# The 16-bit low products of features A, issued once for four steps of a block instead of once for two

## Chip, core and metric

The kernel runs on one core of one Trainium2 chip. The metric is the device time in microseconds (us) of one execution. TensorE (PE in the profile, PEld for its weight loads) multiplies matrices, VectorE (DVE) and ScalarE (ACT) work elementwise, GpSimd (POOL) adds and issues some transfers, and SyncE (SP) issues most transfers. Each engine takes its instructions in its own order.

## Reference

```python
def _attn_ref(x, weight):                  # x: 8 x 4096 x 192, weight: 8 x 7
    w = softmax(weight, axis=-1)           # 7 taps for each head of 24 features
    # causal convolution over the sequence: 6 zeros are padded ahead of it
    out = np.einsum('hk,bskhg->bshg', w, x_unf)
    return out.reshape(B, S, D)

def _moe_ref(x, w_in, w_out, s, b):        # x: 32768 x 192
    h = x @ w_in                           # 192 x 2048
    r = np.maximum(h, 0.0)
    g = s * (r * r) + b
    return g @ w_out                       # 2048 x 192

def reference(x, weight, w_in, w_out, s, b):
    return _moe_ref(_attn_ref(x, weight).reshape(32768, 192), w_in, w_out, s, b)
```

So each token's 192 features are smoothed with seven taps, multiplied out to 2048 hidden features, squared where positive, and multiplied back to 192 features.

## The kernel before

**Tiles.** The 32768 tokens are cut into 32 super-blocks `n` of 1024 tokens, and each of these into two blocks `j` of 512. The 2048 hidden features are eight *steps* `p` of 256 in each block. The 192 features are 128 "features A" and 64 "features B". Precision is kept by splitting numbers into a high and a low part: `sA`, `wA`, `tB`, `wB` hold parts of the smoothed tokens, `W` and `WB` parts of the weights, `qh` and `ql` the high and low part of the squared hidden features.

**One step.** `first(n, j, p)` issues 18 matmuls (L659), nine for each half of the rows, into `h`. ScalarE takes the positive part (L674) and squares it (L681) in `q`; VectorE casts `qh` (L683) and subtracts `ql` (L701; from super-block 3 on, `n >= SCALED`, this is 16 bits wide, two steps in one tile). `second(n, j, p)` multiplies `qh` by the output weights: four matmuls on features B (`acc2`, with `WB`), then eight on features A (`acc1`, with `W`), all on L773. The products of the low part `ql` use a 16-bit copy of the output weights, `halves`, which lies in a buffer named `words`: those of features B, `lows_B` (L758), are issued for all eight steps of a block in its last step, and those of features A (L796) are collected in the list `lows_A` and issued for two steps together, in steps 1, 3, 5 and 7. One step's share of L796 is four matmuls, so a visit has eight. All matmuls of a block on features A add into the same two `acc1` accumulators.

**The order of a block.** `first` runs two to three steps ahead of `second` (`LAG = 2`, with one more at a block's start). Written with F for `first`, S for `second`, A for the low products of features A and B for those of features B, TensorE's order from one block into the next is: S7 B A(6,7) of the last block, F2 F3 S0 S1 A(0,1) F4 S2 F5 S3 A(2,3) F6 S4 F7 S5 A(4,5) of this one, then F0 and F1 of the next block with S6 and S7 of this one between, and so on. Below, F3 or S3 is always step 3 of the block in question.

**What else goes on in a block.** VectorE convolves the tokens of the next super-block, piece by piece between the steps (`accA`, `accB`; L237, L239), splits them (L256, L267, L271, L272), and in the second block (j = 1) of a super-block, ahead of step 3's cast, finds the greatest magnitude of the super-block after next (`peak`, L207, until n = 29, since there are 32). That number goes through two GpSimd transfers (`there`, `t`) and returns to VectorE as `m` (L161), ahead of step 7's cast. VectorE's and ScalarE's orders are those of the program text.

**The end of a block.** After S7 and its low products, ScalarE moves the accumulators out (L810, L813), GpSimd adds the two halves of features B (L814, `oB`) and of features A (L818, `oA`), SyncE moves the upper half of `oB` to the lower partitions (L817, into `oC`), and GpSimd adds this to the other half (L823, `oC`); SyncE stores `oA` and `oC`. The order on GpSimd and SyncE isn't fixed by the text: the scheduler that compiles the program sets it by when it reckons that operands come ready.

Of the kernel before, what the change touches and what calls it, by code (L numbers as in the profile page):

```python
# [44 lines left out]
def conv_attention_then_squared_relu_mlp(  # L45
# [98 lines left out]
    def folded(columns):  # L144

        return columns.rearrange("p (a b) -> p b a", a=2)
# [563 lines left out]
    def accumulators(n, j, p):  # L710
        if p == 0:
            acc[n, j] = [ps_o.tile([P, BLK], F32, name=f"acc{k}") for k in (1, 2, 1, 2)[: 4 if n else 2]]
        return acc[n, j]
# [38 lines left out]
    def lows_B(n, j, to, some):  # L752


        for p in some:
            ql = low_halves.pop((n, j, p))
            for k in range(2):
                nc.tensor.matmul(  # L758
                    to[k * DB :][0:DB], halves[1][:, 2 * p + k, :], ql[:, k, :],
                    start=False, stop=p == NPAIR - 1, skip_group_check=True,  # L760
                )

    def second(n, j, p, qh, ql):
        if (n, j, p) == steps[-1]:
            return last(n, j, qh, ql)
        accs = accumulators(n, j, p)

        ends = [NF - 1, NF - 1 if (n, j) != steps[-1][:2] else NF - 3]

        def both(to, w, f, q, start=False, stop=False):  # L770
            for i in range(2):
                r = slice(i * HB, (i + 1) * HB)
                nc.tensor.matmul(  # L773
                    accs[to + 2 * i], w(f, r), folded(q[r, f % 2, :]),
                    start=start and f == 0, stop=stop and f == ends[i],
                )

        scaled = n >= SCALED
        for f in (2 * p, 2 * p + 1):
            both(1, w_outB, f, qh, start=True, stop=scaled)  # L780
            if not scaled:
                both(1, w_outB, f, ql, stop=True)
        for f in (2 * p, 2 * p + 1):
            both(0, loA, f, qh, start=True)
            both(0, hiA, f, qh)
            if not scaled:
                both(0, hiA, f, ql, stop=True)
        if scaled:
            if p == NPAIR - 1 or (n, j, p + 1) == steps[-1]:
                lows_B(n, j, accs[1], range(p + 1))  # L790
            lows_A.append((p, ql))
            if p % 2 or (n, j, p + 1) == steps[-1]:
                for f, low in ((2 * k + c, low[:, c, :]) for k, low in lows_A for c in range(2)):
                    for i in range(2):
                        r = slice(i * HB, (i + 1) * HB)
                        nc.tensor.matmul(  # L796
                            accs[2 * i], halves[0][r, f, :], low[r],
                            start=False, stop=f == ends[i],
                        )
                lows_A.clear()  # L800
        if p == NPAIR - 1:
            t0 = n * SUP + j * BLK
            early = (n, j) == (1, 0)

            sb = tok_s[n]
            o = {}
            for k, name in ((1, "oB"), (0, "oA")):
                o[k] = outs.tile([P, BLK], F32, name=name)
                o[k + 2] = outs.tile([P, BLK], F32, name=name + "2", bufs=1)
                nc.scalar.activation(  # L810
                    o[k], accs[k], AF.Identity, scale=sb, bias=0.0 if early else bias[:, k : k + 1]
                )
                nc.scalar.activation(o[k + 2], accs[k + 2], AF.Identity, scale=sb)  # L813
            nc.gpsimd.tensor_tensor(o[1], o[1], o[3], op=ALU.add)  # L814

            oC = outs.tile([DB, BLK], F32, name="oC", bufs=1)
            nc.sync.dma_start(oC, o[1][DB:P])  # L817
            nc.gpsimd.tensor_tensor(o[0], o[0], o[2], op=ALU.add)  # L818
            toA, toB = outT[0:P, t0 : t0 + BLK], outT[P:D, t0 : t0 + BLK]
            oB = o[1][0:DB] if early else oC  # L820
            if not early:
                nc.sync.dma_start(toA, o[0])
            nc.gpsimd.tensor_tensor(oB, oC, o[1][0:DB], op=ALU.add)  # L823
            if early:
                unbiased.extend(((o[0], toA, 0), (oB, toB, 2)))
            else:
                nc.sync.dma_start(toB, oB)
            del acc[n, j]
# [14 lines left out]
    def last(n, j, qh, ql):  # L843

        accs = accumulators(n, j, NPAIR - 1)
        sb = tok_s[n]
        uA, uB = upper_sums(accs, sb)
        t0 = n * SUP + j * BLK
        for f in (NF - 2, NF - 1):
            nc.tensor.matmul(  # L850
                accs[1], w_outB(f), folded(qh[:, f % 2, :]), start=False, stop=f == NF - 1
            )
        lows_B(n, j, accs[1], (NPAIR - 1,))
        oB = outs.tile([P, BLK], F32, name="oB")[0:DB]
        nc.vector.scalar_tensor_tensor(
            oB, accs[1][0:DB], sb[0:DB], uB, op0=ALU.mult, op1=ALU.add
        )
        nc.vector.scalar_tensor_tensor(
            oB, accs[1][DB:P], sb[DB:P], oB, op0=ALU.mult, op1=ALU.add
        )  # L860
        nc.sync.dma_start(outT[P:D, t0 : t0 + BLK], oB)
        oA = outs.tile([P, BLK], F32, name="oA")
        for f in (NF - 2, NF - 1):
            for w in (loA, hiA):
                nc.tensor.matmul(
                    accs[0], w(f, slice(0, P)), folded(qh[:, f % 2, :]), start=False, stop=False
                )
        for f in (NF - 2, NF - 1):
            nc.tensor.matmul(
                accs[0], halves[0][:, f, :], ql[:, f % 2, :], start=False, stop=f == NF - 1  # L870
            )
        for k, e in enumerate((nc.scalar, nc.sync)):
            c = slice(k * BLK // 2, (k + 1) * BLK // 2)
            nc.vector.scalar_tensor_tensor(
                oA[:, c], accs[0][:, c], sb, uA[:, c], op0=ALU.mult, op1=ALU.add
            )
            e.dma_start(outT[0:P, t0 + c.start : t0 + c.stop], oA[:, c])
# [93 lines left out]
    steps = [(n, j, p) for n in range(1, NSUP) for j in range(2) for p in range(NPAIR)]  # L971
# [56 lines left out]
    for item in queue:  # L1028
        with in_order(nc.vector):
            second(*item)  # L1030
# [44 lines left out]
```

## Time and profile before

| | |
|---|---|
| median of 3 runs | 2053.38 us (2052.86 to 2054.66) |
| the profiled execution | 2054.64 us, its span 2052.9 us |
| TensorE | busy 2042.1 us, 99% |
| VectorE | busy 1789.1 us, 87% |
| ScalarE | busy 1331.6 us, 65% |
| GpSimd | busy 475.8 us, 23% |
| L796, the moved matmuls | 1852 of this form, busy 241.0 us |

Busy time is the union of an engine's instructions. A matmul's row shows some 376 ns, but the halves run beside each other and overlap, so the pace of the matmuls is read from starts of successive groups. In the timeline a row is a run of like instructions: its start, how long it lasts, the engine, the line, and in brackets how long the engine was idle ahead of it and what ended that.

### The profile page before, as it was taken

The page shows a single profiled execution, that of the slowest core. Times are in us where ns is not written, and L with a number is a line of the kernel's source. Part 1 is how long each engine was busy: PE and PEld are TensorE (multiplying, and loading weights), DVE is VectorE, ACT ScalarE, POOL GpSimd, SP SyncE. Part 2 cuts the span into 40 slices and gives each one's busy share as a digit, 9 for nine tenths or more (in the row PEclk, how much of TensorE's full clock was granted, in tenths as well). Part 3 has the DMA queues.
Part 4 walks back from the last instruction along what each step waited for, and adds up shares of the span by engine and source line. Part 5 has one row for each costly group of instructions (what it writes and reads, how often), then busy time and mean ns, then how long its engine had stood idle before and what let it go on. Part 6 is the DMA issues. An engine that isn't in the chain of part 4 may idle for free.

```text
span 2052.9 us, 43220 instructions
## 1 busy us (share of the span) xinstructions
PE 2042.1 (99%) x18404; PEld 1619.3 (79%) x18404; DVE 1789.1 (87%) x2187; ACT 1331.6 (65%) x1460; POOL 475.8 (23%) x352
## 2 busy tenths in 40 slices
PE   9999999999999999999999999999999999999999
PEld 6789877777777777777777787777777777877776
DVE  9888888888888889888889888898888898888975
ACT  8877866566666665666666656656666666566565
POOL 0013232122231222321222312223212233132210
PEclk9999999999999999999999999999999999999999
DMA  5022222121222222221222222122212222221210
GB/s 196 21 52 77 63 60 63 47 68 45 71 60 50 58 57 58 61 58 49 62 53 71 58 52 58 52 63 60 55 53 60 55 69 59 52 59 47 52 42 19
DMA packets 48561, 121.36 MB, mean 59 GB/s; under 512 B 9200, under 2 KB 9456, under 8 KB 48368
## 3 DMA queue, kind: packets, MB, share of 16 engines
q1 hardware_dynamic: 45824, 114.50, 20.1%
q0 software_dynamic: 2400, 3.97, 1.6%
q8 instruction: 144, 2.36, 0.6%
q14 instruction: 49, 0.40, 0.1%
q10 hardware_dynamic: 144, 0.13, 0.0%
HBM read 35.57 MB, written 25.20 MB: 30 GB/s over the span
## 4 chain that ended last, share of the span: by engine, by line
PE 90%; DVE 4%; DMA 3%; ACT 2%; issue 1%; POOL 0%; SPq 0%; DVEq 0%; POOLq 0%
PE h L659 44%; PE acc L773 31%; PE acc L796 10%; PE acc L758 5%; DMA there<-peak 2%; DMA t<-there 1%; DVE ql L688 1%; ACT q L674 1%; ACT q L681 0%; DVE c L405 0%; DVE t L391 0%; DVE accA L239 0%; DVE qh L683 0%; DVE peak L207 0%; DVE W L411 0%
## 5 line engine op out<-in xcount | busy, mean ns | idle before, releaser
L674 ACT ACTIVATE q<-h 128x1024 f32<-128x1024 f32 x496 | 506.1, 1020 | 585.2 <-PE h L659 570.7
L701 DVE TENSOR_TENSOR ql<-q,qh 128x1024 f16<-128x1024 f32 x464 | 610.9, 1317 | 24.7 <-DVE qh L683 0.5
L681 ACT ACTIVATE q<-q 128x1024 f32<-128x1024 f32 x512 | 543.2, 1061 | 14.3
L773 PE MATMUL acc<-qh,W 64*128 64x512 f32 x3960 | 515.9, 376 | 0.4 <-ACT oA L810 0.3
L683 DVE CAST qh<-q 128x1024 fp32r<-128x1024 f32 x477 | 334.4, 701 | 162.6 <-ACT q L681 156.6
L659 PE MATMUL h<-sA,W 64*128 64x512 f32 x3072 | 461.3, 405 | 2.6 <-DVE W L413 1.7
L773 PEld LDWEIGHTS acc<-qh,W 64*128 64x128 f32 x3960 | 377.2, 186 | 52.7 <-ACT oA L810 0.7
L659 PE MATMUL h<-wA,W 64*128 64x512 f32 x3072 | 416.9, 376 | 0.0
L659 PE MATMUL h<-wB,W 64*128 64x512 f32 x1536 | 413.4, 376 | 0.0
L659 PE MATMUL h<-tB,W 64*128 64x512 f32 x1536 | 413.4, 376 | 0.0
L659 PEld LDWEIGHTS h<-sA,W 64*128 64x128 f32 x3072 | 292.5, 186 | 66.8 <-DVE W L413 2.5
L659 PEld LDWEIGHTS h<-wA,W 64*128 64x128 f32 x3072 | 292.8, 186 | 40.0
L239 DVE SCALAR_TENSOR_TENSOR accA<-xA,taps,accA 128x512 f32<-128x512 f32 x348 | 312.8, 899 | 6.2
L659 PEld LDWEIGHTS h<-tB,W 64*128 64x128 f32 x1536 | 284.7, 186 | 26.7 <-issue 0.2
L773 PE MATMUL acc<-qh,WB 64*128 64x512 f32 x1980 | 304.0, 379 | 1.3 <-DVE qh L683 1.2
L814 POOL TENSOR_TENSOR oB<-oB,oB 128x512 f32<-128x512 f32 x61 | 101.8, 1669 | 874.1 <-ACT oB L810 784.8
L659 PEld LDWEIGHTS h<-wB,W 64*128 64x128 f32 x1536 | 284.7, 186 | 13.5
L796 PE MATMUL acc<-ql,words 64*128 64x512 f16 x1852 | 241.0, 379 | 0.0
L773 PEld LDWEIGHTS acc<-qh,WB 64*128 64x128 f32 x1980 | 186.5, 186 | 32.9 <-DVE qh L683 8.6
L796 PEld LDWEIGHTS <-words 64*128 64x128 f16 x1852 | 72.2, 95 | 119.5 <-issue 64.9
L239 DVE SCALAR_TENSOR_TENSOR accB<-xB,taps,accB 128x512 f32<-128x512 f32 x174 | 161.3, 927 | 3.1
L818 POOL TENSOR_TENSOR oA<-oA,oA 128x512 f32<-128x512 f32 x61 | 113.6, 1862 | 2.8 <-ACT oA L813 2.5
(155 smaller groups left out, 1390.9 us busy)
## 6 DMA issues: line engine op xcount, KB each, us to landing
wA<-sA SPq DMA_DIRECT2D x126, 256.0 KB, 3.4
outT<-oA SPq DMA_DIRECT2D x63, 256.0 KB, 2.4
wB<-tB SPq DMA_DIRECT2D x60, 256.0 KB, 3.4
xA<-in_xA SPq DMA_DIRECT2D x24, 515.0 KB, 3.6
xB<-in_xB SPq DMA_DIRECT2D x32, 259.0 KB, 3.0
oC<-oB SPq DMA_DIRECT2D x61, 128.0 KB, 2.7
outT<-oC SPq DMA_DIRECT2D x60, 128.0 KB, 2.3
words<-in_w SPq DMA_DIRECT2D x7, 768.0 KB, 5.5
```

The source lines that it names most:

```text
L239: nc.vector.scalar_tensor_tensor(acc, src, w[:, k : k + 1], acc, op0=ALU.mult, op1=ALU.add)
L659: nc.tensor.matmul(h[:, i, :], w_in(w, p, chunk[0], rows), folded(chunk[part]), start=start, stop=stop,)
L674: nc.scalar.activation(q, h, AF.Relu, scale=scale)
L681: nc.scalar.activation(q, q, AF.Square)
L683: cast(qh, q)
L688: nc.vector.tensor_tensor(ql, q, qh.bitcast(F32), op=ALU.subtract)
L701: nc.vector.tensor_tensor(ql.rearrange("p f (b a) -> p f b a", a=2), *(v.rearrange("p f (a b) -> p f b a", a=2) for v in (q, qh.bitcast(F3 ...
L758: nc.tensor.matmul(to[k * DB :][0:DB], halves[1][:, 2 * p + k, :], ql[:, k, :], start=False, stop=p == NPAIR - 1, skip_group_check=True,)
L773: nc.tensor.matmul(accs[to + 2 * i], w(f, r), folded(q[r, f % 2, :]), start=start and f == 0, stop=stop and f == ends[i],)
L796: nc.tensor.matmul(accs[2 * i], halves[0][r, f, :], low[r], start=False, stop=f == ends[i],)
L814: nc.gpsimd.tensor_tensor(o[1], o[1], o[3], op=ALU.add)
L818: nc.gpsimd.tensor_tensor(o[0], o[0], o[2], op=ALU.add)
```

## The change

The condition under which `second` issues the collected low products of features A becomes true in steps 3 and 7 of a block, and no longer in 1 and 5; in the very last block it is true in steps 3 and 6 (step 7 has code of its own).

```diff
             lows_A.append((p, ql))
-            if p % 2 or (n, j, p + 1) == steps[-1]:
+            if p % 4 == 3 or (n, j, p + 1) == steps[-1]:
                 for f, low in ((2 * k + c, low[:, c, :]) for k, low in lows_A for c in range(2)):
```

On TensorE, after step 1 of the first block that has 16-bit low parts (n = 3, j = 0), the visit of L796 is gone; the first rows of it, of 16, as the difference of the two orders (`words` is the buffer of the 16-bit weights; the number tells buffers apart):

```order
 L773 MATMUL acc1_2886<-qh_2783,W_104 128x512
-L796 LDWEIGHTS words_2698
-L796 MATMUL acc1_2884<-ql_2727,words_2698 128x512
-L796 LDWEIGHTS words_2698
-L796 MATMUL acc1_2886<-ql_2727,words_2698 128x512
```

So S1 is followed by F4 without A(0,1). The same eight matmuls, with the low tile of steps 0 and 1 (`ql_2727`), now stand after S3, ahead of those of steps 2 and 3 (`ql_2851`):

```order
 L773 MATMUL acc1_2886<-qh_2879,W_104 128x512
 L796 LDWEIGHTS words_2698
+L796 MATMUL acc1_2884<-ql_2727,words_2698 128x512
+L796 LDWEIGHTS words_2698
+L796 MATMUL acc1_2886<-ql_2727,words_2698 128x512
```

The visit after S3 thus has sixteen matmuls, A(0 to 3). Likewise A(4,5) moves from S5 to the end of the block, behind S7 and `lows_B`, as A(4 to 7). TensorE issues as many instructions as before.

On GpSimd, at the end of a block, the difference of the two orders shows two blocks:

```order
 L814 TENSOR_TENSOR oB_3623<-oB_3623,oB2_3624 128x512
+L823 TENSOR_TENSOR oC_3632<-oC_3632,oB_3623 64x512
 L818 TENSOR_TENSOR oA_3627<-oA_3627,oA2_3628 128x512
-L823 TENSOR_TENSOR oC_3632<-oC_3632,oB_3623 64x512
 L814 TENSOR_TENSOR oB_4014<-oB_4014,oB2_4015 128x512
+L823 TENSOR_TENSOR oC_4023<-oC_4023,oB_4014 64x512
 L818 TENSOR_TENSOR oA_4018<-oA_4018,oA2_4019 128x512
-L823 TENSOR_TENSOR oC_4023<-oC_4023,oB_4014 64x512
 L151 DMA there_4068<-peak_4065 128x2x1
 L153 DMA t_4070<-there_4068 128x256
```

The scheduler has put the add of `oC`, which waits for SyncE's transfer of L817, ahead of the add of `oA`, and so in every block. SyncE's store of `oA` (L822) stands behind that of `oC` (L827) accordingly. The orders of VectorE and ScalarE are the same as before.

## The prediction

> **What bounds the kernel now.** I read the page first, then the waits, then the timeline of TensorE and of the other engines over one block.
>
> ```profile
> PE 2042.1 (99%) x18404; PEld 1619.3 (79%) x18404; DVE 1789.1 (87%) x2187; ACT 1331.6 (65%) x1460; POOL 475.8 (23%) x352
> ...
> PEld acc L773 <- DVE qh L683: 8.6, 32, 0.9
> ...
> L207 DVE TENSOR_REDUCE peak<-xA 128x1 f32<-128x1030 f32 x29 | 35.5, 1225 | 0.9
> ```
>
> The first row, busy times, says that TensorE is the bound; it gives no margin, since VectorE's 87% is a mean. The second, of the waits (us in total, times, longest), is the warning: some 30 times TensorE already waits for VectorE's cast `qh`. The third, of the groups, gives a count to compare with: the greatest magnitude is sought 29 times, in blocks j = 1 of n = 1 to 29, and of these 27 have the 16-bit low parts (n = 3 to 29).
>
> The next fence is TensorE's timeline around such a block.
>
> ```profile
> 1001.45 1.03 PE L773 MATMUL acc<-qh,W 64*128 64x512 f32 x8
> 1002.31 0.81 PE L659 MATMUL h<-sA,W 64*128 64x512 f32 x6
> ...
> 1004.25 0.60 PE L773 MATMUL acc<-qh,WB 64*128 64x512 f32 x4
> ...
> 1015.53 1.00 PE L659 MATMUL h<-sA,W 64*128 64x512 f32 x6
> ...
> 1017.66 0.81 PE L659 MATMUL h<-sA,W 64*128 64x512 f32 x6
> ...
> 1021.33 1.03 PE L773 MATMUL acc<-qh,W 64*128 64x512 f32 x8
> 1022.20 1.04 PE L796 MATMUL acc<-ql,words 64*128 64x512 f16 x8
> 1022.89 1.00 PE L659 MATMUL h<-sA,W 64*128 64x512 f32 x6
> ...
> 1025.02 0.59 PE L773 MATMUL acc<-qh,WB 64*128 64x512 f32 x4
> ...
> 1026.31 0.81 PE L659 MATMUL h<-sA,W 64*128 64x512 f32 x6
> ...
> 1028.25 0.64 PE L773 MATMUL acc<-qh,WB 64*128 64x512 f32 x4
> 1028.73 1.03 PE L773 MATMUL acc<-qh,W 64*128 64x512 f32 x8
> 1029.60 1.04 PE L796 MATMUL acc<-ql,words 64*128 64x512 f16 x8
> 1030.29 1.00 PE L659 MATMUL h<-sA,W 64*128 64x512 f32 x6
> ```
>
> F2 starts at 1015.53, F3 at 1017.66, the visit A(0,1) at 1022.20, F4 at 1022.89, S2 at 1025.02, F5 at 1026.31, S3 at 1028.25. S3's first group of four takes 0.48 to the next row's start (1028.25 to 1028.73); eight matmuls at full pace take 0.86 (1001.45 to 1002.31), so four would take 0.43. So S3 waits some 0.05 there, and the next fence says for what: VectorE, ScalarE and GpSimd in the same stretch.
>
> ```profile
> 1015.81 1.70 POOL L814 TENSOR_TENSOR oB<-oB,oB 128x512 f32<-128x512 f32 x1 [25.77 <-ACT oB L810]
> ...
> 1016.28 1.77 DVE L239 SCALAR_TENSOR_TENSOR accB<-xB,taps,accB 128x512 f32<-128x512 f32 x1
> ...
> 1017.47 1.72 POOL L818 TENSOR_TENSOR oA<-oA,oA 128x512 f32<-128x512 f32 x1
> 1017.87 1.02 ACT L674 ACTIVATE q<-h 128x1024 f32<-128x1024 f32 x1 [0.59 <-PE h L659]
> ...
> 1018.52 0.46 SPq L817 DMA_DIRECT2D oC<-oB  x1
> ...
> 1020.01 0.69 DVE L683 CAST qh<-q 128x1024 fp32r<-128x1024 f32 x1 [1.96 <-ACT q L681]
> 1020.81 1.26 DVE L701 TENSOR_TENSOR ql<-q,qh 128x1024 f16<-128x1024 f32 x1
> ...
> 1021.79 1.42 POOL L823 TENSOR_TENSOR oC<-oC,oB 64x512 f32<-64x512 f32 x1 [2.60 <-DMA oC<-oB]
> 1022.00 1.50 DVE L267 CAST hiB<-accB 128x512 fp32r<-128x512 f32 x1
> ...
> 1023.42 0.41 DVE L271 CAST tB<-accB 64x512 fp32r<-64x512 f32 x1
> ...
> 1025.72 1.23 DVE L207 TENSOR_REDUCE peak<-xA 128x1 f32<-128x1030 f32 x1
> ...
> 1027.46 0.68 DVE L683 CAST qh<-q 128x1024 fp32r<-128x1024 f32 x1
> ...
> 1029.86 0.75 DVE L239 SCALAR_TENSOR_TENSOR accA<-xA,taps,accA 128x512 f32<-128x512 f32 x1
> ...
> 1041.52 0.42 DVE L161 TENSOR_REDUCE m<-t 128x1 f32<-128x256 f32 x1 [1.61 <-DMA t<-there]
> ```
>
> VectorE has nothing to do for 1.96 ahead of step 2's cast, at 1020.01: that cast waits for ScalarE, and ScalarE for F2 (1017.87, `<-PE h`). From there to the end of step 3's cast (1027.46 + 0.68 = 1028.14) it works without a pause: the low part, the split of features B, the two searches for the greatest magnitude. S3 starts 0.11 behind that end. So a chain from F2 over ScalarE and 8.1 us of VectorE ends at the very moment when TensorE, coming from F2 by its own way, arrives at S3. Step 3 of a j = 1 block is where margin is missing.
>
> **The change, part by part.**
>
> *A(0,1) leaves its place ahead of S3.* From S1's group on features A to S2 it is 1021.33 to 1025.02 = 3.69 with the visit; the same stretch without one is 1001.45 to 1004.25 = 2.80. The visit costs 0.89; eight matmuls at full pace cost 0.86, so that 0.02 or 0.03 go to switching between the kinds. TensorE thus reaches S3 0.88 sooner. F2 and F3 stand ahead of the moved visit and start no sooner, so the chain from F2 to the cast isn't shortened: all 0.88 becomes waiting, on top of the 0.05. The eight matmuls are then done after S3, at their old price.
>
> *A(4,5) leaves its place after S5* for the block's end. What lies between (F0 and F1 of the next block, S6, S7) is offered 0.88 sooner than without any stall; after a stall of that size at S3 it comes where it came before. S7's cast stands behind `m` (1041.52, a wait of 1.61 for the transfer that began with `peak`); that chain too hangs on VectorE's time after F2, so it keeps its place relative to S3's cast, and S7 adds nothing. F2 of the next block starts behind A(4 to 7), eight matmuls later than it did after S7: here the stall becomes span.
>
> *Two visits fewer in each of 58 blocks*: 116 x 0.02 = 2.3 us less; by the rows' rounding between 0 and 3.5.
>
> *The adds on GpSimd.* With a GpSimd add running, VectorE's instruction that starts meanwhile takes about one us more: L239 takes 1.77 beside the add of `oB` and 0.75 with nothing beside it (1016.28 and 1029.86), the cast `hiB` 1.50 beside the add of `oC`, while the cast of the same 512 columns in `tB` takes 0.41 (1022.00 and 1023.42). The price of an add that meets a busy VectorE is 1.02 to 1.09. Before, the add of `oA` (1017.47 to 1019.19) ran mostly while VectorE was idle and cost the chain nothing. Now it stands behind `oC`'s, which waits for SyncE's transfer: issued at 1018.52 and usable at 1021.79. Relative to F2, the end of the eight-matmul-longer tail puts `oB`'s add and this transfer 0.86 earlier, so `oC`'s add comes at about 1020.9, is held up by `ql` until 1022.07, and ends by 1023.2 as before (it costs `hiB` the same 1.1). The add of `oA` follows, at 1023.5 and for over a us, where VectorE is in the split of features B. Its cover, the 1.96 of idle time, is gone. The bounds: 0 if it happens to lie beside instructions that aren't held up, 1.1 if it costs a full turn; I take 1.05, the mean of the two rows, as what it meets is the casts and subtractions that rows show held up. So step 3's cast ends 1.05 later relative to F2.
>
> The skill bears on the lower bound. The Trainium skill (SBUF — State Buffer, Who interferes with whom) says that VectorE and GpSimd share one pair of ports as an exclusive lock, that a two-input VectorE instruction or a cast in the two-port mode is blocked for the whole other instruction, and that a `tensor_reduce` on trn2 never is. The 1.50 against 0.41 agrees with the first part; no row here shows an add beside a reduction. By that rule an add that fell wholly beside the two searches would be free, and the sum would be that of the first rival.
>
> *The second block j = 0.* There VectorE is behind for another reason, and has more room:
>
> ```profile
> 1056.82 0.69 DVE L683 CAST qh<-q 128x1024 fp32r<-128x1024 f32 x1
> ...
> 1059.79 0.60 PE L773 MATMUL acc<-qh,WB 64*128 64x512 f32 x4
> ```
>
> Step 3's cast ends at 1057.51 and S3 starts at 1059.79: 2.28 of margin against 0.88. VectorE is busy there through all three adds already, so their order costs little. No stall.
>
> *The other engines.* SyncE's store of `oA` goes out later by the wait for `oC`, ahead of the exchange of `tB` halves, which waits for VectorE anyway; ScalarE's moves out of the accumulators start with the longer tail's end and keep their distance to F2. The sixteen-matmul visits need `ql` of steps 3 and 7 later than before. Nothing.
>
> *The sum.* Per super-block n = 3 to 29: 0.88 + 1.05 = 1.93 of new waiting; 27 x 1.93 = 52.1 us. Less 2.3 for the switches: +49.8. On the profiled execution's 2054.64 that is 2104.4; this execution lies 1.3 above the median of the three runs (2053.38), so the median to expect is 2103.2. I say 2103.5.
>
> **The rivals.**
>
> *The add of `oA` costs the chain nothing* (it meets the two searches, or idle time). For it: the transfer of `oC` needs only land 2 us later for the add to meet the reductions at 1025.72. Against it: 3.27 from issue to use at 1018.52, and nothing that lengthens it. Then 27 x 0.88 - 2.3 = +21.5, 2075. Chance 0.15.
>
> *Not slower: VectorE comes sooner as well.* If step 3's cast weren't tied to F2 (if VectorE had work in hand instead of the 1.96 pause), it would move up with TensorE, and only the switches would show: -2.3, that is 2051. It decides in favour when the pause at 1020.01 closes and at least 1.9 of margin appears at S3; what closes it would be an earlier F2, and F2 stands behind sixteen matmuls now. Chance 0.04. With a partial gain that just offsets the 2.3: within 0.2% (4 us, about what a measurement can tell from no change), 0.03.
>
> *Worse: the stalls spread.* F6 and F7 come 1.93 later relative to F2, and with them steps 6 and 7 on ScalarE; step 7's cast waits for `m` now, but if ScalarE, the m-transfer or a further held-up instruction takes that role, each costs up to another add's turn, 1.05 x 27 = 28: 2115 to 2132. Against it: `m` ends its wait at 1041.52 with VectorE idle, so step 7's input is long there. Chance 0.10.
>
> **How the numbers follow.** The forecast's case, both costs in full or the add's cost by half or more (2089 to 2113), has 0.68. The range is to leave out the two small cases below and most of the worse one: from 2072, under the first rival, to 2115. Its share is 0.68 + 0.15 and a little of the worse one. Faster 0.04, within 0.2% 0.03, slower 0.93.
>
> **What would show it.** In the trace after: L773 `qh,WB` of step 3 in j = 1 blocks with some 1.9 of idle TensorE ahead of it, ended by VectorE's `qh`, 27 times, some 50 us in the row of the waits that has 8.6 now; the row of TensorE's busy share near 97%; the add of `oA` (L818) beside a `tB` cast or subtraction that takes 1.4 to 1.8 in place of 0.41 or 0.68; the pause ahead of step 2's cast still near 2 us. The prediction is wrong if S3 finds its cast ready (the chain moved up), if the add of `oA` lies elsewhere (half the waiting), or if S7 or a j = 0 block has waits of its own.

## The result, and the profile after

The changed kernel takes 2107.79 us (median of 4 runs, 2105.65 to 2109.76) where the kernel before took 2054.02 (median of 4, 2052.86 to 2056.20): a ratio of 1.0264, interval 1.0251 to 1.0277, or 53.8 us more. The profiled execution of it has a span of 2103.9 us against 2052.9.

The page's busy times:

```profile
PE 2048.5 (97%) x18404; PEld 1624.9 (77%) x18404; DVE 1810.2 (86%) x2187; ACT 1331.7 (63%) x1460; POOL 448.1 (21%) x352
```

From the waits, the two rows of TensorE for VectorE's cast (weight loads and matmuls apart; us in total, times, longest), and the wait of `m`:

```profile
PEld acc L773 <- DVE qh L683: 59.5, 35, 2.3
PE acc L773 <- DVE qh L683: 46.3, 28, 1.9
DVE m L161 <- DMA t<-there: 36.1, 27, 1.9
```

The weight loads waited 8.6 us before and wait 59.5 now; 51 us is what the span grew by. VectorE's busy time grew by 21 while its work is the same.

The timeline of one j = 1 block after the change, from F2 to the visit behind S3:

```profile
1036.00 1.90 PE L796 MATMUL acc<-ql,words 64*128 64x512 f16 x16
1037.55 1.00 PE L659 MATMUL h<-sA,W 64*128 64x512 f32 x6
1042.03 0.69 DVE L683 CAST qh<-q 128x1024 fp32r<-128x1024 f32 x1 [2.80 <-ACT q L681]
1042.92 2.31 POOL L823 TENSOR_TENSOR oC<-oC,oB 64x512 f32<-64x512 f32 x1 [4.24 <-DMA oC<-oB]
1044.01 1.50 DVE L267 CAST hiB<-accB 128x512 fp32r<-128x512 f32 x1
1045.20 1.45 POOL L818 TENSOR_TENSOR oA<-oA,oA 128x512 f32<-128x512 f32 x1
1045.44 1.49 DVE L271 CAST tB<-accB 64x512 fp32r<-64x512 f32 x1
1047.64 0.42 DVE L271 CAST tB<-accB 64x512 fp32r<-64x512 f32 x1
1050.56 0.68 DVE L683 CAST qh<-q 128x1024 fp32r<-128x1024 f32 x1
1051.29 0.70 PE L773 MATMUL acc<-qh,WB 64*128 64x512 f32 x4 [1.74 <-DVE qh L683]
1052.70 1.90 PE L796 MATMUL acc<-ql,words 64*128 64x512 f16 x16
```

F2 starts at 1037.55 and step 2's cast at 1042.03, 4.48 later; before it was 1015.53 and 1020.01, also 4.48. So the chain still hangs on F2, in this block and by the median. From that cast's start to the end of step 3's cast it took 8.13 before (1020.01 to 1028.14) and 9.21 now (1042.03 to 1051.24). The difference, 1.08, is one row: a `tB` cast of 1.49 beside the late add of `oA`, where the next one with nothing beside it takes 0.42. S3's matmuls start 0.05 behind the cast's end, after 1.74 of idle time on TensorE.

Not every block looks like this one. In 16 of the 27 the add of `oA` holds up a `tB` cast, which takes 1.4 to 1.5. In 9 others the add of `oC` begins a moment before the subtraction `ql` (L701) instead of behind it, and `ql` takes 3.4 to 3.6 where it takes 1.27 otherwise: it stands behind both adds, and `hiB` and `tB` then take 0.41 each. Cast to cast is 9.0 to 9.4 in either case, so an add costs about the same turn wherever it meets VectorE's work. (The order of the adds changed from super-block 3 on; the four blocks ahead of that have the old one.)

For the comparisons below I took the starts of F2, S3, S7 and the next block's F2, and the two casts, out of each trace, and their medians over the 27 blocks with j = 1 and n = 3 to 29 (us; "cast to cast" is from the start of step 2's to the end of step 3's):

| kernel | cast to cast | F2 to S3 | S3 to S7 | S7 to next F2 | F2 to next F2 |
|---|---|---|---|---|---|
| before | 8.12 | 12.72 | 14.76 | 3.92 | 31.40 |
| after | 9.22 | 13.76 | 14.80 | 4.79 | 33.34 |
| f0_before_late_m | 8.13 | 12.72 | 14.76 | 3.92 | 31.40 |
| f1_after_late_m | 9.21 | 13.75 | 14.80 | 4.79 | 33.34 |
| f2_after_oA_first_late_m | 8.12 | 12.66 | 14.80 | 4.79 | 32.24 |
| f3_before_oC_first_late_m | 9.20 | 13.74 | 14.81 | 3.92 | 32.48 |
| f4_only_A45_oA_first_late_m | 8.12 | 12.72 | 13.87 | 4.79 | 31.38 |
| e1_after_oA_first | 8.13 | 12.66 | 16.17 | 4.89 | 33.71 |
| e2_before_oC_first | 9.21 | 13.74 | 16.11 | 4.03 | 33.88 |
| e3_only_A01 | 8.12 | 12.66 | 16.24 | 4.03 | 32.93 |
| e4_only_A45 | 9.21 | 13.74 | 16.17 | 6.53 | 36.43 |
| e6_after_early_peak | 7.95 | 12.49 | 14.80 | 4.79 | 32.07 |
| e7_before_early_peak | 7.04 | 12.72 | 14.71 | 3.92 | 31.35 |
| e8_after_early_peak_oA_first | 7.04 | 11.84 | 14.69 | 4.79 | 31.32 |

A block is 1.94 longer after the change: 27 x 1.94 = 52.4. F2 to S3 has lost a visit and is 1.04 longer all the same.

### The profile page after: what moved, and what is told of

Its sections match the earlier page's. It is cut to its first block, busy times and chain, and to the rows that moved or that the text cites. A ratio compares the mean times of both kernels' runs of the same rounds, so it can differ in the third digit from the quotient of the medians.

```text
span 2103.9 us, 43216 instructions
## 1 busy us (share of the span) xinstructions
PE 2048.5 (97%) x18404; PEld 1624.9 (77%) x18404; DVE 1810.2 (86%) x2187; ACT 1331.7 (63%) x1460; POOL 448.1 (21%) x352
## 4 chain that ended last, share of the span: by engine, by line
PE 79%; DVE 11%; issue 4%; ACT 4%; DMA 1%; POOL 0%; DVEq 0%; SPq 0%; POOLq 0%; ACTq 0%
PE h L659 38%; PE acc L773 27%; PE acc L796 10%; PE acc L758 5%; DVE peak L207 2%; DVE tB L272 2%; DVE qh L683 2%; ACT q L681 2%; ACT q L674 2%; DVE hiB L267 1%; DVE tB L271 1%; DVE ql L688 1%; DMA there<-peak 0%; DVE c L405 0%; DVE accA L239 0%
## 5 line engine op out<-in xcount | busy, mean ns | idle before, releaser
L701 DVE TENSOR_TENSOR ql<-q,qh 128x1024 f16<-128x1024 f32 x464 | 634.0, 1366 | 24.7 <-DVE qh L683 0.5
L683 DVE CAST qh<-q 128x1024 fp32r<-128x1024 f32 x477 | 371.1, 778 | 193.5 <-ACT q L681 187.6
L659 PE MATMUL h<-sA,W 64*128 64x512 f32 x3072 | 438.9, 391 | 1.7 <-ACT q L674 0.9
L239 DVE SCALAR_TENSOR_TENSOR accA<-xA,taps,accA 128x512 f32<-128x512 f32 x348 | 264.3, 760 | 6.2
L773 PEld LDWEIGHTS acc<-qh,WB 64*128 64x128 f32 x1980 | 184.3, 186 | 84.5 <-DVE qh L683 59.5
L796 PE MATMUL acc<-ql,words 64*128 64x512 f16 x1852 | 220.8, 378 | 0.0
L796 PEld LDWEIGHTS <-words 64*128 64x128 f16 x1852 | 81.1, 94 | 120.7 <-issue 39.1
L823 POOL TENSOR_TENSOR oC<-oC,oB 64x512 f32<-64x512 f32 x60 | 89.4, 1489 | 199.6 <-issue 163.5
```

What stands on the lines that cost most here:

```text
L239: nc.vector.scalar_tensor_tensor(acc, src, w[:, k : k + 1], acc, op0=ALU.mult, op1=ALU.add)
L659: nc.tensor.matmul(h[:, i, :], w_in(w, p, chunk[0], rows), folded(chunk[part]), start=start, stop=stop,)
L683: cast(qh, q)
L701: nc.vector.tensor_tensor(ql.rearrange("p f (b a) -> p f b a", a=2), *(v.rearrange("p f (a b) -> p f b a", a=2) for v in (q, qh.bitcast(F3 ...
L773: nc.tensor.matmul(accs[to + 2 * i], w(f, r), folded(q[r, f % 2, :]), start=start and f == 0, stop=stop and f == ends[i],)
L796: nc.tensor.matmul(accs[2 * i], halves[0][r, f, :], low[r], start=False, stop=f == ends[i],)
```

## The experiments

Every run was compared with the kernel before on the same chip. That kernel's own time differs between the groups of runs: 2054 where the change was measured, 2092.5, 2051.6 and 2064.5 in the three below, each of which ran on a chip of its own. The first group shows a cause.

### The two halves and the order of the adds, one by one

`e1_after_oA_first` holds GpSimd to the order of before: the adds, as they stand in the text, under a context that keeps an engine's text order.

```diff
-            nc.gpsimd.tensor_tensor(o[1], o[1], o[3], op=ALU.add)
...
+            with in_order(nc.gpsimd):
+                nc.gpsimd.tensor_tensor(o[1], o[1], o[3], op=ALU.add)
...
```

> The changed kernel with GpSimd held to the order of before (add of oA ahead of that of oC; SyncE's stores accordingly). Theory: two separate prices, 0.88 us per super-block for taking A(0,1) from ahead of S3 and some 1.05 for the add of oA that now meets a busy VectorE. Only the first is left here: 27 x 0.88 - 2 = +21 to +23, 2075 to 2077. Rival (the order on GpSimd does nothing, all comes from TensorE's order): as the changed kernel, 2106 to 2110. Rival (the late add is the whole cause): 2052 to 2056.

`e2_before_oC_first` is the kernel before with the add of `oA` written behind that of `oC`, under the same context; SyncE's store of `oA` moves behind it.

```diff
-            nc.gpsimd.tensor_tensor(o[0], o[0], o[2], op=ALU.add)
...
+                nc.gpsimd.tensor_tensor(oB, oC, o[1][0:DB], op=ALU.add)
+                nc.gpsimd.tensor_tensor(o[0], o[0], o[2], op=ALU.add)
...
```

> The kernel before with GpSimd's adds in the order of the changed kernel (oC ahead of oA), TensorE's order untouched. Theory: step 3's cast in j = 1 blocks ends 1.05 later and S3 has next to no margin, so 27 x 1.05 = +28, 2080 to 2084, and L818 lies beside a tB cast or subtraction of 1.4 us or more. Rival (the order on GpSimd does nothing): 2054, no more than 2 away.

`e3_only_A01` and `e4_only_A45` do one half of the change each.

```diff
-            if p % 2 or (n, j, p + 1) == steps[-1]:
+            if p in (3, 5, 7) or (n, j, p + 1) == steps[-1]:
```

> Of the change only A(0,1) moved to S3; A(4,5) stays after S5. Here the orders of GpSimd and SyncE are those of before. Theory: 27 x 0.88 - 58 x 0.02 = +22 to +23, 2076 to 2077, with the wait ahead of S3 near 0.9. Rival (the longer tail of the block is what costs): 2053 to 2055.

```diff
-            if p % 2 or (n, j, p + 1) == steps[-1]:
+            if p in (1, 3, 7) or (n, j, p + 1) == steps[-1]:
```

> Of the change only A(4,5) moved to the block's end; A(0,1) stays after S1. The scheduler here puts the add of oC ahead of that of oA, as in the changed kernel. Theory: the move itself costs nothing, the order of the adds 1.05 per super-block: 27 x 1.05 - 1 = +27, 2080 to 2082. Rival (the move of A(4,5) alone is harmless and so is the order of the adds): 2053. Rival (the longer burst at the block's end stalls the next block as well): 2090 or more, with waits ahead of S0 or S2.

Measured, beside a kernel before of 2092.53 us: e1 2109.70 (ratio 1.0077, 1.0055 to 1.0099), e2 2117.14 (1.0115, 1.0093 to 1.0137), e3 2093.72 (1.0002, 0.9991 to 1.0012), e4 2170.76 (1.0370, 1.0343 to 1.0398). No time came out as expected, and e3's +1 and e4's +78 not even as a difference. The timelines of e3 tell why; first VectorE's, then TensorE's waits in the same block, then its row in the list of waits:

```profile
1043.09 0.68 DVE L207 TENSOR_REDUCE peak<-xB 128x1 f32<-128x518 f32 x1
...
1059.11 0.42 DVE L161 TENSOR_REDUCE m<-t 128x1 f32<-128x256 f32 x1 [2.94 <-DMA t<-there]
```

```profile
1044.42 0.70 PE L773 MATMUL acc<-qh,WB 64*128 64x512 f32 x4 [0.65 <-DVE qh L683]
...
1060.62 0.70 PE L773 MATMUL acc<-qh,WB 64*128 64x512 f32 x4 [0.36 <-DVE qh L683]
```

```profile
DVE m L161 <- DMA t<-there: 80.7, 30, 3.3
```

From the end of the second search (1043.77) to `m` it is 15.34 here. In the profile before, that search ran from 1026.86 for 0.68 and `m` started at 1041.52, 13.98 later; over the 27 blocks the medians are 15.38 and 13.64. From the end of that search to the landing of `t` it is 15.3 by the median in each of these four runs, against 13.7 in the profile before, so the two GpSimd transfers took 1.6 us longer and step 7's cast came late and S7 had to wait for it (the row at 1060.62) as well as S3 (1044.42). S3 to S7 is 16.24 in the table, against 14.76. The kernel before must have had this wait too; it has no profile from this chip. If its S7 came when e3's did, 12.66 + 16.24 = 28.90 after F2, a block of it took 28.90 + 4.03 = 32.93 in place of 31.40, and 27 x 1.53 = 41 us is just what separates its 2092.5 from the 2051.6 of the next group. The transfers fit as well: to the landing of `t` it is 13.3 to 13.5 in that group, where the kernel before takes 2051.6, 13.7 where it takes 2054, 14.0 to 14.2 in the third group, where it takes 2064.5, and 15.3 here. Where S7 waits for `m`, and `m` hangs on F2, a stall at S3 costs nothing more: e3 was free there. What then counts is the end of the block, from S7 on, and the time at which the searches run: e2 makes the searches 1.08 later (27 x 1.08 = 29; measured 24.6), e1 makes the end 0.86 longer (27 x 0.86 - 2 = 21; measured 17.2).

e4 does both, about 52, and has 26 more. They are in the granted clock. The windows of e4 around one S7:

```profile
core 0: us, PE busy (x) PEld busy (x) DVE busy (x) ACT busy (x) POOL busy (x), PEclk, DMA share, GB/s
286.00:291.00 5.00, 3.83 (x36) 3.03 (x32) 1.63 (x3) 3.61 (x4) 0.15 (x1) 1.00 0.51 121
291.00:296.00 5.00, 3.65 (x20) 2.29 (x22) 4.86 (x9) 1.63 (x2) 4.28 (x3) 0.66 0.04 14
296.00:301.00 5.00, 5.00 (x48) 3.18 (x46) 4.76 (x6) 2.13 (x3) 1.53 (x2) 1.00 0.49 122
```

And from its timeline, S7 in the second of these windows:

```profile
292.35 1.22 PE L773 MATMUL acc<-qh,WB 64*128 64x512 f32 x4 [2.52 <-DVE qh L683]
293.36 1.92 PE L773 MATMUL acc<-qh,W 64*128 64x512 f32 x8
```

TensorE stood still for 2.52 us, from 289.83 on, and from 292.04 the granted clock was one half for 3.41 us, a mean of 0.66 over the five microseconds; eight matmuls lasted 1.92 instead of 1.03. The trace has 18 such spells in e4's blocks, each 3.41 us long and so worth up to 1.7: at most 31 us, about what was missing. The Trainium skill (TensorE: Matmul & The Clock Gate, What's actually happening) gives windows of about 3.4 us and half the clock after an idle one; the spell's length agrees, the 2.52 of idle time that sufficed is less than a window.

The fourteen traces say which pauses suffice. The spells of a trace start a whole number of times 3.413 us apart. With each trace cut into stretches of that grid, from the first j = 1 block with n = 3 to the end of the last, all 24 stretches in which TensorE was idle for 1.85 us or more were followed by a spell, and none of the others was, of which the most idle had 1.84. So a pause shorter than a stretch costs clock when enough of it falls into one stretch: that is why 1.85 us can suffice in one block and pauses up to 1.9 pass in others.

### The same with the wait for m taken out

To read the two prices whatever the transfers take, `m` is used one step later.

```diff
                 with headed():
                     start_tokens(n + 1)
+                if SCALED <= n + 1 < NSUP:
+                    with behind(nc.vector):
+                        tok[n + 1].scale()
...
-            elif p == 7:
-                with behind(nc.vector):
-                    ahead[n + 2].scale()
```

This edit alone is `f0_before_late_m`; the others have it on top of the changed kernel (f1), of e1 (f2) and of e2 (f3).

> The kernel before with one edit: VectorE's use of the returned maximum (m, L161 and what follows) stands behind step 7's cast and low part, ahead of the next block's step 0, so that the transfers from peak to m get some 2 us more. The runs of the first four kernels, with a kernel before of 2092, suggest that this transfer takes longer in some sessions and then S7, not S3, ends last. Theory: this kernel doesn't wait for m any longer and takes 2050 to 2054 whatever the transfer's time. Rival (something else made those runs longer): it stays with the kernel before, within 0.3%, also where that takes 2092.

> The changed kernel with the same late m. Theory: both stalls ahead of S3 in full against the kernel with late m alone: 27 x (0.88 + 1.0) less 2 = +49, 2100 to 2104, with nothing waiting for m. Rival (the stalls of the changed kernel hang on m): it comes near 2053 or stays above 2107.

> The changed kernel, GpSimd in the order of before, late m. Theory: A(0,1)'s 0.88 alone, against the kernel with late m alone 27 x 0.88 - 2 = +22, 2073 to 2077. Rival (the order of the adds does nothing): as the changed kernel with late m, 2100 to 2104.

> The kernel before, oC added ahead of oA, late m. Theory: the add's price alone, 27 x 1.0 = +27 against the kernel with late m alone, 2077 to 2082. Rival (the order of the adds does nothing): as the kernel with late m alone.

Measured, beside a kernel before of 2051.58: f0 2051.51 (ratio 0.9998, 0.9988 to 1.0007), f1 2104.18 (1.0258, 1.0243 to 1.0273), f2 2071.74 (1.0098, 1.0083 to 1.0113), f3 2081.06 (1.0144, 1.0129 to 1.0159). In this group the transfers were the shortest (13.3 to 13.5), and f0 shows no gain: its time is as expected, but whether it would hold it where the kernel before takes 2092 is left open. (Two kernels of the next group, e7 and f4, hardly wait for `m` either, and take 2050 where the kernel before takes 2064.5.) The other three are as the theory has them: f1 0.2 above its range, f2 1.3 under its own, and f3 inside. A(0,1) costs 20.2, the order of the adds 29.5, together 49.7, and both at once 52.6. The difference goes with the granted clock of f1's four executions: 2101.88 us at a mean of 1.000, 2103.70 at 0.999, 2104.65 at 0.998 and 2107.79 at 0.996. The first, at full clock, is 50.3 above the kernel before. The waits for VectorE's cast, of f1, f2 and f3 in that order:

```profile
PEld acc L773 <- DVE qh L683: 57.7, 28, 2.3
```

```profile
PEld acc L773 <- DVE qh L683: 26.9, 27, 1.2
```

```profile
PEld acc L773 <- DVE qh L683: 34.9, 29, 1.4
```

Each part has 27 to 29 waits, and they add up: f0 has 4.8 us of such waits, f2 22.1 and f3 30.1 more, together 57.0, where f1 has 57.7. The rivals by which the adds' order did nothing, or was everything, fall.

### What holds VectorE up, and whether both stalls can be had away

`e6_after_early_peak`, `e7_before_early_peak` and `e8_after_early_peak_oA_first` move the two searches ahead of the split of features B, in the changed kernel, in the kernel before, and in e1.

```diff
-            elif p == 3:
-                with behind(nc.vector):
-                    ahead[n + 2].peak()
...
             queue.append((n, j, p, *low))
+            if j == 1 and p == 2 and SCALED <= n + 2 < NSUP:
+                with behind(nc.vector):
+                    ahead[n + 2].peak()
```

> The changed kernel with the two searches for the greatest magnitude (peak, L207) moved from behind the split of features B to ahead of it, right behind step 2's low part. VectorE's work between F2 and step 3's cast is the same; what changes is that the adds of oC and oA now run beside the searches. Theory (a search isn't held up by an add, the casts and subtractions are): the chain gets shorter by some 1.1 for oC and 0.6 to 1.1 for oA, S3 waits 0.1 to 0.5 in place of 1.9, and m comes 3 us sooner: 2052 to 2062. Rival (an add holds up a search as well): 2100 to 2108 as in the changed kernel.

> The kernel before with the searches in the same early place. Theory: about 1.1 more margin ahead of S3, where 0.05 was lost, and m no longer late: 2048 to 2051 beside a kernel before of 2052, more of a gain if the transfers are slow in that session. Rival (searches are held up too): as the kernel before, within 0.1%.

> The changed kernel with the early searches and GpSimd in the order of before: both stalls taken away, the two visits fewer per block kept. Theory: S3 waits 0 to 0.2, so 58 x 2 x 0.02 = 2 us below the kernel before with early searches: 2047 to 2051, the fastest of all. Rival (the grouping by four costs something of its own, as by the longer burst): 2053 or more.

The last one, `f4_only_A45_oA_first_late_m`, is the half that moves A(4,5), with the adds in the order of before and `m` late, without the early searches.

> Of the change only A(4,5) moved to the block's end, GpSimd in the order of before, late m. Theory: this half of the change costs nothing by itself and saves 58 switches: 1 us below the kernel with late m alone, 2049 to 2053. Rival (the longer end of a block delays the next block beyond its eight matmuls, or S7 waits for its cast now): 27 x 0.5 = 13 or more above.

Measured, beside a kernel before of 2064.54: e6 2086.40 (2081.48 to 2087.26; ratio 1.0097, 1.0083 to 1.0111), e7 2050.05 (0.9930, 0.9918 to 0.9943), e8 2056.60 (2051.81 to 2057.77; 0.9956, 0.9943 to 0.9969), f4 2050.29 (0.9931, 0.9918 to 0.9945). The timeline of e7, VectorE and GpSimd:

```profile
1018.54 1.27 DVE L701 TENSOR_TENSOR ql<-q,qh 128x1024 f16<-128x1024 f32 x1
1019.42 1.53 POOL L823 TENSOR_TENSOR oC<-oC,oB 64x512 f32<-64x512 f32 x1 [2.49 <-DMA oC<-oB]
1019.71 1.23 DVE L207 TENSOR_REDUCE peak<-xA 128x1 f32<-128x1030 f32 x1
1020.85 0.69 DVE L207 TENSOR_REDUCE peak<-xB 128x1 f32<-128x518 f32 x1
1021.45 0.43 DVE L267 CAST hiB<-accB 128x512 fp32r<-128x512 f32 x1
```

The add of `oC` runs beside the first search, which takes 1.23 as it did with nothing beside it, and `hiB` takes 0.43 in place of 1.50. Cast to cast shrinks from 8.12 to 7.04, by just that 1.1. So the rule of the Trainium skill (SBUF — State Buffer, Who interferes with whom) that the prediction named is borne out: a search isn't held up by an add, a cast is. In e6 the second add, of `oA`, meets the second search and then `hiB`:

```profile
1028.56 0.70 DVE L207 TENSOR_REDUCE peak<-xB 128x1 f32<-128x518 f32 x1
1028.63 1.27 POOL L818 TENSOR_TENSOR oA<-oA,oA 128x512 f32<-128x512 f32 x1
1029.16 1.03 DVE L267 CAST hiB<-accB 128x512 fp32r<-128x512 f32 x1
```

`hiB` loses 0.6 here: the add outlasts the search. I had expected S3 to wait 0.1 to 0.5, and e6 at 2052 to 2062; it missed by 20 us and more. S3 still waits in it, 33.8 us in all where 59.5 were in the changed kernel. The table's median of 7.95 hides two kinds of blocks. In 13 of the 27, as here, cast to cast is 7.64 and S3 waits 0.2 to 0.3. In 10 it is 9.2 to 9.4, as in the changed kernel, and S3 waits 1.7 to 1.9. One of these:

```profile
644.44 1.28 POOL L823 TENSOR_TENSOR oC<-oC,oB 64x512 f32<-64x512 f32 x1 [3.94 <-issue]
644.67 3.39 DVE L701 TENSOR_TENSOR ql<-q,qh 128x1024 f16<-128x1024 f32 x1
645.69 1.26 POOL L818 TENSOR_TENSOR oA<-oA,oA 128x512 f32<-128x512 f32 x1
```

The add of `oC` begins 0.23 ahead of `ql` here, not behind it. The subtraction stands behind both adds and takes 3.39 in place of 1.27, and the searches come too late to shield anything. In the ten blocks the add is 0.04 to 0.23 ahead; in the 13 it begins with `ql` or up to 1.0 behind it. With all blocks of the length of the 13 (31.76) the profiled execution would be 21.6 us shorter, some 2060 and in the range. The mechanism was right, but it hung on which of two instructions started first, which the expectation didn't ask.

e7 came out as expected, e8 more than 5 us above its range in the median, though its profiled execution, at 2051.81, lies near it. The grouping by four is not faster than the kernel before with the same edit: 2056.60 against 2050.05, so by the medians the rival (2053 or more) has it. The trace names another cause than the grouping. The margin ahead of S3 is 0.32 in the profiled execution (F2 to S3 is 11.84 where e7 has 12.72, with the same chain). In four blocks the add of `oC` begins 0.02 to 0.21 ahead of `ql`, `ql` takes 2.2 to 2.4, and S3 waits 0.5 to 0.7; the four cost 3.3 us. In 15 others the add begins less than 0.2 behind `ql`, where e7 has at least 0.58 in all blocks but one. That the slower executions have more such blocks fits this but was not shown: only the fastest was profiled. f4 says that moving A(4,5) alone costs nothing: S3 to S7 is 0.89 shorter, S7 to the next F2 0.87 longer, and the block 31.38 against 31.40.

The fastest versions are e7 and f4, 0.7% below the kernel before in their group and not to be told apart. In a comparison like that of f0, where the kernel before has little to wait for, no such gain was measured.

## Why the prediction was right, point by point

- *S3 of a j = 1 block has no margin, and 0.88 becomes waiting.* Right. F2 to step 2's cast stayed 4.48; f2 shows the price alone, 0.84 of a block, which is 0.88 less two switches.
- *The add of `oA` costs 1.05.* Right, and a little small: 1.08 to 1.10 by cast to cast, 29.5 us by f3 where 27 x 1.05 = 28.4 was reckoned.
- *The place.* Right in 16 of 27 blocks, where a `tB` cast beside the add takes 1.4 to 1.5, in the range of 1.4 to 1.8. In 9 both adds came ahead of `ql` instead, which the prediction didn't see; that the price was the same there is luck as far as its working goes.
- *Two switches fewer, 2.3 us.* Of the right size: F2 to the next F2 is 31.38 in f4 with one visit fewer and 31.32 in e8 with two, against 31.40 and 31.35. As a time it was not separated from the differences between the groups.
- *S7 adds nothing.* Right in the result: S3 to S7 is 14.80 after and 14.76 before. It hung on a transfer time that was 1.6 longer in the first group of experiments, where S7 was the bound. The prediction saw that `m` stands ahead of step 7's cast but took one block's 13.98 as a constant; that the change was measured where this held was luck. Even there S7 waited now and then: 3.1 us in eight blocks of the kernel before, 1.4 in seven of the changed one.
- *The j = 0 blocks.* Right: margin at S3 there was 1.3 to 2.2 after the change, but for the first one.
- *The sum.* +49.8 reckoned, +53.8 measured. The adds' price accounts for 1.1 of the 4.0. A term was left out: a stall of nearly 2 us now and then costs the clock as well. The changed kernel's windows around one such stall:

```profile
1690.00:1698.00 8.00, 6.15 (x60) 5.06 (x56) 7.88 (x10) 4.47 (x5) 2.21 (x3) 1.00 0.42 117
1698.00:1703.00 5.00, 5.00 (x30) 2.79 (x32) 4.86 (x6) 0.30 (x1) 0.43 (x1) 0.66 0.01 0
```

TensorE was idle for 1.85 and then ran at a mean of 0.66 for five microseconds, 1.7 lost. The profiled execution has this once in its blocks, f1's three times. The profiled execution is also the shortest of the four, and only 51.0 longer than that of the kernel before; the longest, at 2109.76, has the lowest granted clock, 0.997 against 0.998. The rest isn't settled.

- *The rivals.* "The add costs nothing" fell with f3. "Not slower" fell: the pause ahead of step 2's cast didn't close, it grew to 2.80. "The stalls spread" didn't happen in the result, but its mechanism was seen in e4.

## What to carry to other kernels

An engine at 99% leaves no slack to fill, so work that is moved on it matters by what it used to cover: look for the consumer behind it that another engine feeds just in time, and ask whether that feeder's start moves too. A few instructions moved on one engine can make the scheduler reorder another: read the order of every engine, and price each moved instruction by what it now runs beside, and by which of the two starts first. Where several chains end within 0.1 us of each other, which of them bounds can differ from one group of runs, or one chip, to another, so first give the chain that varies more room, and then measure the others.

## What the runs showed of the hardware that was not expected

- Spells of half the granted clock, 3.41 us each, follow a grid of 3.413 us. Idle time of TensorE of 1.85 us within one stretch of it was followed by a spell (24 of 24), 1.84 or less never was. So the stalls of the changed kernel, mostly 1.5 to 1.9 us, cost clock once in 27, the longer ones of e4 18 times.
- The way of a small result through memory and back by two GpSimd transfers took 13.3 to 13.5 us by the median in one group of runs, 13.7, 14.0 to 14.2 and 15.3 in the others, with the same instructions; between 2051 and 2092 us for the kernel before, this is the only cause that the traces point to. Whether it is the chip or the time of the run isn't known.
- VectorE's `tensor_reduce` took 1.23 us beside a GpSimd add and without one, while a cast of 512 columns took 1.49 to 1.50 beside one and 0.41 to 0.43 without. A subtraction that began 0.2 us behind an add took 3.39 in place of 1.27, past the end of that add and of the next.
